# Attention scores on half arrays: K and Q loaded once, one bank for h, three for the attention's outputs

## The chip, the cores and the metric

The kernel runs on one core of one Trainium2 chip. The metric is the device time of one execution in microseconds (us). TensorE (PE) multiplies matrices, VectorE (DVE), ScalarE (ACT) and GpSimd (POOL) work on elements, and SyncE (SP) issues the DMA transfers. Each engine takes its instructions in a fixed order and stops at the first whose operands or buffers are not ready, so a late instruction holds all that stands behind it on its engine.

## The reference

Three layers follow one another. The first is attention over 4 batches of 8 heads, 576 positions and 64 columns a head. Scores below the row's maximum minus `tau` are dropped before the softmax. The two others are dense pairs of matrix products on 2304 tokens, 512 to 2048 to 512, each with its own activation between the products.

```python
scores = scale * np.matmul(q, k.transpose(0, 1, 3, 2))
thresh = np.max(scores, axis=-1, keepdims=True) - tau
scores = np.where(scores >= thresh, scores, -1000000000.0)
attn = np.exp(scores - np.max(scores, axis=-1, keepdims=True))
attn = attn / (np.sum(attn, axis=-1, keepdims=True) + 1e-09)
x = np.matmul(attn, v)            # rows of one token joined over the heads
...
h = x @ w_in                      # first layer: 512 -> 2048
sp = np.where(h > 20.0, h, np.log1p(np.exp(np.minimum(h, 20.0))))
x = (h * np.tanh(sp)) @ w_out     # 2048 -> 512
...
h = x @ w_in2                     # second layer
out = (h * np.clip(h + 3.0, 0.0, 6.0) / 6.0) @ w_out2
```

## The kernel before

**Parts of a number.** Accuracy beyond one 16-bit or one fp32r product is had by parts: an operand is written as a high part and the rest of it, a low part. For the dense layers both parts are f16, and a product is three matmuls (high times high, high times low, low times high; `TERMS`, line 36). For the scores the parts are fp32r.

**Attention.** Heads go in 16 pairs (4 batches, 4 pairs). A pair has four full query tiles of 128 rows for each head and one tail tile, which holds the last 64 rows of both heads: 9 score tiles of 128 x 576, so 144 in all; we count progress in these "heads". K and Q arrive with the 64 columns of a head stacked twice over the 128 partitions (`_stack`, line 1358). In `pair` (971) ACT makes the high parts (`k_hi` 991, `q_hi` 984), DVE the low part of K (`k_lo` 994, `kl` in the trace), and POOL the low part of Q into the other 64 rows (`q_lo` 987; the helper `sub`, line 330, holds the instruction). One matmul over 128 rows is then (high Q + low Q) times one part of K, so a head needs two matmuls for each of two halves of 288 columns (`scores`, 1044): 8 for a full tile of two heads, 8 for a tail tile.

**From scores to outputs.** For each head DVE takes the row maximum (`peak` 1066), ACT the exponential (`exp` 1076) and the threshold (`threshold` 1071), DVE masks (`mask` 1079, the last reader of the scores), ACT and POOL make the f16 parts (`p_hi` 1084, `p_lo` 1087), a DMA transposes them (1092), and PE multiplies with V (`pv` 1098). Scores lie in a ring `s` of two tiles of two PSUM banks each; a head takes one tile, and the next scores may enter it when its mask is done. Outputs and turned tiles share the ring `aux`, two banks.

**Dense work in the gaps.** When the first half of a batch is through, the first product of the first layer for that block of 256 tokens can begin (`inner` 679, `gemm1` 655): 8 groups of 24 matmuls (line 661, `h_g`), each into one of two banks of the ring `h`, emptied by `he_t` on ACT or DVE (`take`, 706) and stored. A block has 192 such matmuls. The weights of this product are converted during the first batch (`one_conversion` 493: lines 519 and 524 on DVE, 511 and 330 on POOL). The second product and the second layer (lines 825, 661 and 837) fill PE after the attention.

**What sets the order.** Nothing is scheduled on the chip. `Plan` (131) keeps a clock for every engine while the program is built, takes the task that can start first (within `WINDOW`, by due time) and writes its instructions down. The due times come from constants (`STEP`, `PREP_AHEAD`, `MOE_LAG`, `EASE`), the durations from literals in the tasks. They say nothing of the chip's time; they only set the order.

```python
r_s = ring("s", ps_a, BANKS["s"], [P, 2, 512])
r_aux = ring("aux", ps_a, BANKS["aux"], [P, FULL])
r_rk = ring("rk", ap, 1, [P, 2, S])
...
deps = [ql[j], kl] if c < NQ else [*ql, kl]
held = [s[j], qs, kd, kld]
```

Of the kernel before, what the change touches and what calls it, by code (L numbers as in the profile page):

```python
# [21 lines left out]
P = 128  # L22
# [19 lines left out]
STEP = 2.55  # L42
START = 7.2
PV_OFF = 6.17
PREP_AHEAD = 2.45
CONV_STEP = 1.5
CONV_AT = 3.0
LATE_STEP = 4.0
# [4 lines left out]
MOE_LAG = 8.26  # L53
RATE = 1.32
NX = 3
FLIP = 1.61
ALPHA = {"act": 3.07, "pe": 10.98}
# [5 lines left out]
MERGE_HI = False  # L63
MERGE_LO = True
# [5 lines left out]
PIECE = 4  # L70
LAG = 4
BANKS = {"s": 2, "aux": 2, "h": 2}
# [4 lines left out]
EASE = {"mk": -1.41, "ph": 1.68, "pl": -3.92, "tr": -1.06, "ex": 0.6, "s": -3.68, "th": -5.15}  # L77
P_LO = ("pool",)
EXPAND = {"act": 1.15}
BUFS = {"e": 3, "p16": 3}  # L80
LATE = {"gs": 5, "hl": 2, "xl": 2, "yl": 1, "h": 2, "y": 2}
WINDOW = {"pe": 0.05, "dve": 0.05, "act": 0.02, "pool": 0.15, "sp": 0.22}


class Ring:
# [11 lines left out]
    def when(self):  # L97
        return min(self.free)[0] if self.free else None
# [32 lines left out]
class Plan:  # L131
# [153 lines left out]
def fused_kernel(ctx: ExitStack, tc, q, k, v, tau, w1i, w1o, w2i, w2o, out):  # L285
# [393 lines left out]
    def inner(blk, early, at=None, gap=0.0):  # L679
# [19 lines left out]
        for fp in range(NG):  # L699
# [219 lines left out]
    r_qs = [Ring("qs", lambda i, name, k=k: qts[2 * k + i], 2) for k in range(2)]  # L919
# [51 lines left out]
    def pair(n, begin, values, sets):  # L971
# [8 lines left out]
        qs, kd, kld = Buf(r_qs[sets]), Buf(r_kd[sets]), Buf(r_kld[sets])  # L980
# [26 lines left out]
        a = prep({"act": 1.155}, lambda e: q_hi(slice(0, 2)), [lq], [rq, qs], "qh")
        for j in range(2):
            ql.append(prep(both(S), lambda e, j=j: q_lo(e, j), [a], [rq, qs], f"ql{j}_"))
        kl = prep({"dve": 1.42}, k_lo, [kh], [rk, kd, kld], "kl")  # L1010
# [15 lines left out]
        def query_tiles(t, c, o, i):  # L1026
# [17 lines left out]
            def scores(j):  # L1044
                if c < NQ:
                    q0 = j * TAIL + c * P
                    st = qs.tile[:, j, q0 : q0 + P]
                    terms = [(st, kd.tile[:, j]), (st, kld.tile[:, j])]
                else:
                    flat = qs.tile.rearrange("p a n -> p (a n)")  # L1050
                    terms = [
                        (flat[:, q0 : q0 + P], k.tile[:, jj])
                        for jj, q0 in enumerate((FULL, S))
                        for k in (kd, kld)
                    ]
                for half in range(2):
                    for m, (lh, rh) in enumerate(terms):
                        mm(  # L1058
                            s[j].tile[:, half, :HALF],
                            lh,  # L1060
                            rh[:, half * HALF : (half + 1) * HALF],
                            start=m == 0,
                            stop=m == len(terms) - 1,
                        )
# [50 lines left out]
            pks, exs = [], []  # L1115
            for j in heads:
                deps = [ql[j], kl] if c < NQ else [*ql, kl]
                held = [s[j], qs, kd, kld]
                a = go(
                    {"pe": 0.56 if c < NQ else 1.08}, lambda e, j=j: scores(j), deps + [prev[0]],  # L1120
                    held, "s", j,
                )
                prev[0] = a
                a = go({"dve": 0.75}, lambda e, j=j: peak(j), [a], [s[j], neg], "pk", j)
# [29 lines left out]
            a = go({"sp": 0.7}, transpose, parts, [p16, pt], "tr", w - 1, 1.0 * w, 0.0, [prev[2]])  # L1154
# [159 lines left out]
    r_hp.grow(maker(ps2, "hp", [P, 2 * BLK], F32), LATE["h"])  # L1314
# [93 lines left out]
```

## Time and profile before

| what | us |
|---|---|
| median of 3 runs (1085.86 to 1089.76) | 1089.45 |
| the profiled execution | 1089.44 |
| its span, first to last instruction | 1087.7 |
| PE busy | 968.7 |
| DVE busy | 604.3 |
| ACT busy | 605.1 |
| POOL busy | 469.2 |

The profiled execution lasts 1.7 us longer than its span, and it is as long as the median, so a sum made against the span's stages can be set beside the runs as it stands. The shares of busy time are averages over stages that differ: attention with its preparation until 453 us, a first product that runs out until 503 us, and then dense products alone. Waits are read stage by stage.

### The profile page before, as it was taken

The page shows a single profiled execution, that of the slowest core. Times are in us where ns is not written, and L with a number is a line of the kernel's source. Part 1 is how long each engine was busy: PE and PEld are TensorE (multiplying, and loading weights), DVE is VectorE, ACT ScalarE, POOL GpSimd, SP SyncE. Part 2 cuts the span into 40 slices and gives each one's busy share as a digit, 9 for nine tenths or more (in the row PEclk, how much of TensorE's full clock was granted, in tenths as well). Part 3 has the DMA queues.
Part 4 walks back from the last instruction along what each step waited for, and adds up shares of the span by engine and source line. Part 5 has one row for each costly group of instructions (what it writes and reads, how often), then busy time and mean ns, then how long its engine had stood idle before and what let it go on. Part 6 is the DMA issues. An engine that isn't in the chain of part 4 may idle for free.

```text
span 1087.7 us, 21597 instructions
## 1 busy us (share of the span) xinstructions
PE 968.7 (89%) x8839; PEld 784.4 (72%) x8839; DVE 604.3 (56%) x1068; ACT 605.1 (56%) x982; POOL 469.2 (43%) x408
## 2 busy tenths in 40 slices
PE   2447688898999986979999999999999999999997
PEld 1436577787899875868888888886666667666663
DVE  7778997777787779757679678621211111111110
ACT  6637777787788778546676559522322322223322
POOL 3859766466565658634433025512222222222221
PEclk9856789998999998999999999999999999999999
DMA  6867679999999898966576967410100100100001
GB/s 258 209 172 175 139 191 238 221 229 252 195 219 218 179 227 171 239 236 235 192 233 231 335 230 265 140 40 1 58 29 11 40 30 11 40 20 20 20 1 39
DMA packets 199394, 162.87 MB, mean 150 GB/s; under 512 B 174080, under 2 KB 174080, under 8 KB 194176
## 3 DMA queue, kind: packets, MB, share of 16 engines
q1 hardware_dynamic: 199296, 161.51, 55.7%
q8 instruction: 69, 1.13, 0.4%
q14 instruction: 29, 0.24, 0.1%
HBM read 90.18 MB, written 28.84 MB: 109 GB/s over the span
## 4 chain that ended last, share of the span: by engine, by line
PE 71%; DMA 11%; DVE 8%; POOL 4%; ACT 3%; issue 2%; SPq 0%; ACTq 0%; POOLq 0%; DVEq 0%
PE h_g L661 19%; PE y_y L825 17%; PE y_y L837 17%; DMA pt_tr<-p_ph 9%; PE hp_g L661 9%; PE s_s L1058 4%; PE aux_pv L1106 4%; DVE e_ex L1080 2%; POOL p_ph L330 2%; DVE nm_pk L1067 1%; POOL qs L330 1%; DMA v_lv<-in_v 1%; ACT e_ex L1077 1%; DMA rq_lq<-in_q 1%; DMA raw_lr<-in_moe_w_in 1%
## 5 line engine op out<-in xcount | busy, mean ns | idle before, releaser
L661 PEld LDWEIGHTS <-w 128*128 128x128 f16 x3456 | 333.5, 98 | 66.9 <-issue 5.8
L330 POOL TENSOR_TENSOR p_ph<-e_ex,p_ph 128x128 f16<-128x128 f32 (+3 forms) x160 | 195.2, 1242 | 110.3 <-ACT p_ph L1085 69.0
L330 POOL TENSOR_TENSOR gs_h<-hl_r,gs_h 128x512 f16<-128x512 f32 x72 | 83.5, 1159 | 286.2 <-ACT gs_h L800 286.2
L837 PE MATMUL y_y<-w,gs_h 128*128 128x512 f16 x864 | 201.7, 379 | 0.0
L825 PE MATMUL y_y<-gs_h,w 128*128 128x256 f16 x1728 | 191.7, 273 | 0.0
L661 PE MATMUL h_g<-x_fl,w 128*128 128x256 f16 x1536 | 187.6, 275 | 3.2 <-ACT he_t L709 2.4
L825 PEld LDWEIGHTS <-w 128*128 128x128 f16 x1728 | 168.4, 98 | 19.3
L837 PEld LDWEIGHTS <-gs_h 128*128 128x128 f16 x864 | 84.5, 98 | 82.0
L800 ACT ACTIVATE gs_h<-hl_r 128x512 f16<-128x512 f32 x72 | 45.3, 629 | 172.0 <-PE y_y L837 155.4
L1067 DVE TENSOR_REDUCE nm_pk<-s_s 128x1 f32<-128x576 f32 x144 | 105.8, 751 | 35.3 <-PE s_s L1058 34.4
L1080 DVE SCALAR_TENSOR_TENSOR e_ex<-s_s,thr_th,e_ex 128x576 f32<-128x576 f32 x144 | 111.6, 810 | 15.0 <-ACT thr_th L1072 11.1
L1106 PE MATMUL aux_pv<-vh,pt_tr 128*128 128x65 f16 (+1 forms) x1296 | 91.1, 207 | 29.8 <-DMA pt_tr<-p_ph 28.1
L1077 ACT ACTIVATE e_ex<-s_s,nm_pk 128x576 f32<-128x576 f32 x144 | 104.1, 732 | 18.4 <-DVE nm_pk L1067 16.3
L784 DVE SCALAR_TENSOR_TENSOR hl_r<-hl_r,f,h_g 128x512 f32<-128x512 f32 x36 | 26.9, 747 | 156.2 <-ACT hl_r L778 156.2
L1106 PEld LDWEIGHTS <-pt_tr 128*128 128x128 f16 x2016 | 83.8, 105 | 37.6 <-DMA pt_tr<-p_ph 33.3
L1085 ACT ACTIVATE p_ph<-e_ex 128x576 f16<-128x576 f32 x144 | 95.6, 680 | 25.7 <-DVE e_ex L1080 18.6
L784 DVE SCALAR_TENSOR_TENSOR hl_r<-hl_r,f,hp_g 128x512 f32<-128x512 f32 x36 | 26.9, 746 | 145.3 <-ACT hl_r L778 145.3
L661 PE MATMUL h_g<-xl_x,w 128*128 128x256 f16 x864 | 104.3, 273 | 0.0
L661 PE MATMUL hp_g<-xl_x,w 128*128 128x256 f16 x864 | 103.0, 273 | 0.0
L1058 PE MATMUL s_s<-kda_kh,qs 128*128 128x288 f32 x200 | 68.5, 357 | 26.8 <-DVE e_ex L1080 18.3
L1058 PEld LDWEIGHTS s_s<-kda_kh,qs 128*128 128x128 f32 x200 | 43.2, 216 | 37.0 <-POOL qs L330 14.9
L804 DVE SCALAR_TENSOR_TENSOR gs_h<-hp_e,fscales,gs_h 128x512 f16<-128x512 f32 x72 | 52.6, 744 | 25.8 <-ACT gs_h L798 25.6
(321 smaller groups left out, 1297.0 us busy)
## 6 DMA issues: line engine op xcount, KB each, us to landing
hd<-he_t SPq DMA_DIRECT2D x36, 512.0 KB, 3.3
hl_l<-hd SPq DMA_DIRECT2D x36, 512.0 KB, 4.5
raw_lr<-in_moe_w_in SPq DMA_DIRECT2D x16, 1024.0 KB, 5.5
raw_lr<-in_moe_w_out SPq DMA_DIRECT2D x16, 1024.0 KB, 6.6
rk_lk<-in_k SPq DMA_DIRECT2D x16, 576.0 KB, 5.2
rq_lq<-in_q SPq DMA_DIRECT2D x16, 576.0 KB, 5.1
raw_lw<-in_moe_w_out SPq DMA_DIRECT2D x8, 1024.0 KB, 7.3
v_lv<-in_v SPq DMA_DIRECT2D x16, 320.0 KB, 4.6
```

Source lines behind the costliest of these rows:

```text
L330: engine[e].tensor_tensor(dst, a, b, ALU.subtract)
L661: mm(hv[:, j, :], wj[:, wl, c * P : (c + 1) * P], x.tile[:, c, xl, :], start=j == 0 and n == 0, stop=j == 1 and n == 11, skip_group_check= ...
L784: nc.vector.scalar_tensor_tensor(half(g), half(g), wsc[2]["f"][:, fp : fp + 1], h.tile, ALU.min, ALU.mult)
L804: nc.vector.scalar_tensor_tensor(s.tile[:, 1], gv(), fs[:, fp : fp + 1], s.tile[:, 0], ALU.mult, ALU.subtract)
L825: mm(yv[:, h, :], wt[m2][f // 2][:, f % 2, wl, c * P : (c + 1) * P], gs[fp].tile[:, gl, f % 2, :], start=fp == 0 and n == 0, stop=fp == NG ...
L837: mm(y.tile[:, j], gs[fp].tile[:, gl, f % 2, j * P : (j + 1) * P], wt[m2][f // 2][:, f % 2, wl, :], start=fp == 0 and n == 0, stop=fp == N ...
L1058: mm(s[j].tile[:, half, :HALF], lh, rh[:, half * HALF : (half + 1) * HALF], start=m == 0, stop=m == len(terms) - 1,)
L1067: nc.vector.tensor_reduce(neg.tile[:, j : j + 1], sv(j), AX.XY, ALU.max, negate=True)
L1077: nc.scalar.activation(ev(j), sv(j), AF.Exp, bias=neg.tile[:, j : j + 1])
L1080: nc.vector.scalar_tensor_tensor(ev(j), sv(j), thr.tile[:, j : j + 1], ev(j), ALU.is_ge, ALU.mult)
L1085: nc.scalar.activation(p16.tile[:, js, :S], e_.tile[:, js], AF.Copy)
L1106: mm(ov[:, dst, :d], pt.tile[:, j, ch, :], part.tile[:, src, vc, :], start=i == j == ch == 0 and part is vh, stop=j == w - 1 and ch == 8, ...
```

## The change

K and Q are loaded once (128 partitions, the two heads of a pair above each other) instead of twice. The parts now lie side by side as columns of one tile: `qs[:, 0]` and `qs[:, 1]` are the high and the low Q of both heads, `kd[:, 0]` and `kd[:, 1]` the same of K. A score matmul of a full tile reads 64 partitions, the upper ones for one head and the lower ones for the other, and `TERMS` makes three products of it (the product of the two low parts goes). The matmuls of the two heads alternate. A tail tile keeps matmuls over 128 partitions, on a Q of which each head's half is zero elsewhere: three terms, two halves, six matmuls. Both heads' scores are one task, which takes both tiles of `s`.

Around it: K is scaled in place on ACT, its low part may be made on POOL or DVE, the raw K and Q have two buffers each, `h` has one bank during the attention (a second one is added after it), `aux` three. The constants of the plan are new.

```diff
-STEP = 2.55
+STEP = 2.33
-PREP_AHEAD = 2.45
+PREP_AHEAD = 3.29
-MOE_LAG = 8.26
+MOE_LAG = 3.41
...
-BANKS = {"s": 2, "aux": 2, "h": 2}
+BANKS = {"s": 2, "aux": 3, "h": 1}
...
-    r_rq = ring("rq", ap, 1, [P, 2, S])
-    r_rk = ring("rk", ap, 1, [P, 2, S])
+    r_rk = ring("rk", ap, BUFS["r"], [P, S])
+    r_qs = [ring("qs" + "ab"[k], (ap, ep)[k], 2, [P, 2, QW], F32R) for k in range(2)]
     r_kd = [ring("kd" + "ab"[k], (ap, ep)[k], 2, [P, 2, S], F32R) for k in range(2)]
-    r_kld = [ring("kld" + "ab"[k], (ap, ep)[k], 2, [P, 2, S], F32R) for k in range(2)]
...
+        def load_q(e):
+            for j, r in enumerate(side):
+                nc.sync.dma_start(out=rq.tile[r, : S - j * TAIL], in_=q[n][r, : S - j * TAIL])
+            nc.sync.dma_start(out=rq.tile[D:, S:], in_=q[n][D:, FULL:])
+        def q_hi(e):
+            nc.scalar.activation(qs.tile[:, 0], rq.tile, AF.Copy)
+        def q_lo(e):
+            sub(e, qs.tile[:, 1], rq.tile, qs.tile[:, 0].bitcast(F32))
+        def k_scale(e):
+            nc.scalar.activation(rk.tile, rk.tile, AF.Copy, scale=qscale)
         def k_hi(e):
-            nc.scalar.activation(kd.tile, rk.tile, AF.Copy, scale=qscale)
+            nc.scalar.activation(kd.tile[:, 0], rk.tile, AF.Copy)
         def k_lo(e):
-            nc.vector.scalar_tensor_tensor(
-                kld.tile, rk.tile, qscale, kd.tile.bitcast(F32), ALU.mult, ALU.subtract
-            )
+            sub(e, kd.tile[:, 1], rk.tile, kd.tile[:, 0].bitcast(F32))
...
-            def scores(j):
-                if c < NQ:
-                    q0 = j * TAIL + c * P
-                    st = qs.tile[:, j, q0 : q0 + P]
-                    terms = [(st, kd.tile[:, j]), (st, kld.tile[:, j])]
+            def scores(e):
...
+                cols = slice(c * P, (c + 1) * P)
                 for half in range(2):
-                    for m, (lh, rh) in enumerate(terms):
+                    for m, (qi, ki) in enumerate(TERMS):
+                        for j, r in enumerate(side):
+                            mm(
+                                s[j].tile[:, half, :HALF],
+                                qs.tile[r, qi, cols],
+                                kd.tile[r, ki, half * HALF : (half + 1) * HALF],
+                                start=m == 0,
+                                stop=m == 2,
+                            )
...
+            prev[0] = scored = go(
+                {"pe": S_COST}, scores, [ql, kl, prev[0]], [*s, qs, kd], "s"
+            )
             for j in heads:
...
     r_hp.grow(maker(ps2, "hp", [P, 2 * BLK], F32), LATE["h"])
+    r_h.grow(maker(ps2, "hx", [P, 2 * BLK], F32), 2 - BANKS["h"])
```

The order moves at three places. The first is PE at a full score tile. In the names, `s_s2_3_0` is pair 2, tile 3, head 0; in the changed kernel the digit before the last number tells the head. Before, the two heads stand behind each other:

```order
L1106 MATMUL aux_pv1_2_0_1_1206<-vh1_132,pt_tr1_2_1_1_1124 128x65
L1058 MATMUL s_s2_3_0_0_1249<-kdb_kh2_1_300,qs2_134 128x288
L1058 MATMUL s_s2_3_0_0_1249<-kldb_kl2_2_361,qs2_134 128x288
...
L1058 MATMUL s_s2_3_1_0_1257<-kdb_kh2_1_300,qs2_134 128x288
L1058 MATMUL s_s2_3_1_0_1257<-kldb_kl2_2_361,qs2_134 128x288
...
L1106 LDWEIGHTS pt_tr1_3_1_1_1197
```

In the changed kernel, at tile 1 of pair 6:

```order
L668 MATMUL h_g20_0_0_0_1_1991<-x_fl0_0_2_504,w0_2_155 128x256
L1074 MATMUL s_s6_1_0_0_2032<-kdb_kh6_1_1391,qsb_qh6_1_1383 128x288
L1074 MATMUL s_s6_1_0_1_2033<-kdb_kh6_1_1391,qsb_qh6_1_1383 128x288
...
L1074 MATMUL s_s6_1_0_1_2033<-kdb_kh6_1_1391,qsb_qh6_1_1383 128x288
L668 LDWEIGHTS w0_3_156
L668 MATMUL h_g30_0_0_0_1_2047<-x_fl0_0_2_504,w0_3_156 128x256
```

The matmuls of the two heads (`s_s6_1_0_0` and `s_s6_1_0_1`) now alternate, each with 64 rows of the same K and Q tiles, 12 in one run where there were 8.

The second is DVE between the masks (`e_ex`) of the 11th and 12th head and the next row maximum (`nm_pk3_0`), where the fourth pair comes in. `cvt` is a weight conversion, `kldb_kl3` the low part of K. Before:

```order
L1080 SCALAR_TENSOR_TENSOR e_ex2_1_0_2_524<-s_s2_1_1_0_515,thr_th2_1_0_1_530,e_ex2_1_0_2_524 128x576
L937 TENSOR_REDUCE vt_vm0_1_1_293<-v_lv2_1_0_496 128x1
...
L524 SCALAR_TENSOR_TENSOR cvt_c0_1__1_412<-raw_lr0_1_0_177,cvt_c0_1__1_412 128x1024
L519 SCALAR_TENSOR_TENSOR cvt_c0_2__1_588<-raw_lr0_2_0_491,cvt_c0_2__1_588 128x1024
L995 SCALAR_TENSOR_TENSOR kldb_kl3_2_633<-rk_lk3_0_375,qscale_84,kdb_kh3_1_433 128x1152
L524 SCALAR_TENSOR_TENSOR cvt_c0_2__1_588<-raw_lr0_2_0_491,cvt_c0_2__1_588 128x1024
L1016 SCALAR_TENSOR_TENSOR vlb_vl3_3_671<-v_lv3_0_0_169,vs_ve0_1_184,vh3_140 128x640
L1177 TENSOR_SCALAR den_dt2_0_2_676<-aux_pv2_0_0_1_593 128x4
L1067 TENSOR_REDUCE nm_pk3_0_0_1_679<-s_s3_0_0_0_666 128x1
```

In the changed kernel:

```order
L1096 SCALAR_TENSOR_TENSOR e_ex2_1_0_2_566<-s_s2_1_0_0_544,thr_th2_1_0_1_570,e_ex2_1_0_2_566 128x576
L1096 SCALAR_TENSOR_TENSOR e_ex2_1_0_2_566<-s_s2_1_0_1_545,thr_th2_1_0_1_570,e_ex2_1_0_2_566 128x576
L531 SCALAR_TENSOR_TENSOR cvt_c0_1__1_349<-raw_lr0_1_0_185,cvt_c0_1__1_349 128x1024
L371 TENSOR_REDUCE top0_144<-aux_zp0_2_1_581 128x1
L408 TENSOR_SCALAR top0_144<-top0_144 128x1
L409 TENSOR_SCALAR sc0_145<-top0_144 128x1
L412 TENSOR_SCALAR sc0_145<-sc0_145 128x1
L1083 TENSOR_REDUCE nm_pk3_0_0_1_636<-s_s3_0_0_0_585 128x1
```

Of 16 instructions between the mask and the row maximum, with four conversion steps and the low part of K, five are left, with one conversion step; the low part of K stands on POOL.

The third is PE between two groups of the first product, `h_g50` and `h_g60` (weights `w0_5`, `w0_6`). Before, at block 1:

```order
L1106 MATMUL aux_pv6_0_0_1_2326<-vh2_136,pt_tr6_1_1_1_2319 128x65
L661 LDWEIGHTS w0_5_160
L661 MATMUL h_g50_0_0_1_1_2397<-x_fl0_2_2_1154,w0_5_160 128x256
...
L661 LDWEIGHTS w0_6_161
L661 MATMUL h_g60_0_0_1_1_2488<-x_fl0_2_2_1154,w0_6_161 128x256
...
L1058 MATMUL s_s4_3_0_0_2507<-kda_kh4_1_937,qs0_126 128x288
```

In the changed kernel, at block 0:

```order
L668 MATMUL h_g50_0_0_0_1_2217<-x_fl0_0_2_504,w0_5_158 128x256
L1233 MATMUL aux_fl5_0_1_2277<-ident_75,xn_dn5_0_2_2265 128x128 x2
L1122 LDWEIGHTS pt_tr6_0_1_1_2148
L1122 MATMUL aux_pv6_0_0_1_2280<-vh2_136,pt_tr6_0_1_1_2148 128x65
...
L668 LDWEIGHTS w0_6_159
L668 MATMUL h_g60_0_0_0_1_2314<-x_fl0_0_2_504,w0_6_159 128x256
...
L1074 MATMUL s_s4_2_0_0_2322<-kda_kh4_1_941,qsa_qh4_1_935 128x288
```

Before, the next group followed the last matmul of the one before at once, into the other bank. Now a turned tile (`aux_fl5`) and a whole product with V (`aux_pv6`, 28 matmuls) stand between them, while the one bank is emptied.

## Rows read from the trace of the kernel before

**Rows 1.** Page, busy time of the engines: busy us (share) x instructions

```profile
PE 968.7 (89%) x8839; PEld 784.4 (72%) x8839; DVE 604.3 (56%) x1068; ACT 605.1 (56%) x982; POOL 469.2 (43%) x408
```

**Rows 2.** Windows: stage, length, busy us (x instructions) PE PEld DVE ACT POOL, clock, DMA, GB/s

```profile
0.00:184.00 184.00, 109.48 (x1049) 94.97 (x1050) 153.14 (x262) 121.87 (x199) 122.63 (x112) 0.81 0.77 194
184.00:375.00 191.00, 176.52 (x2194) 162.01 (x2192) 146.33 (x259) 153.92 (x280) 115.34 (x97) 0.97 1.02 220
375.00:503.00 128.00, 104.01 (x1137) 91.44 (x1136) 96.20 (x192) 84.56 (x142) 75.85 (x63) 0.96 0.83 209
503.00:1000.00 497.00, 497.00 (x3952) 385.77 (x3950) 198.17 (x344) 221.49 (x329) 137.69 (x123) 1.00 0.33 114
```

**Rows 3.** Windows of line 1080 alone, the masks on DVE: busy us (x masks)

```profile
0.00:184.80 184.80, 37.30 (x48) 0.82 0.77 194
184.80:375.00 190.20, 54.97 (x71) 0.97 1.02 220
```

**Rows 4.** Timeline of DVE, 50 to 71 us: start us, us, engine line operation, idle before

```profile
50.35 0.76 DVE L1067 TENSOR_REDUCE nm_pk<-s_s 128x1 f32<-128x576 f32 x1 [0.20 <-PE s_s L1058]
...
65.07 2.31 DVE L995 SCALAR_TENSOR_TENSOR kldb_kl<-rk_lk,qscale,kdb_kh 128x1152 fp32r<-128x1152 f32 x1
67.30 2.18 DVE L524 SCALAR_TENSOR_TENSOR cvt_c__1_588<-raw_lr,cvt_c__1_588 128x1024 uint32<-128x1024 uint32 x1
...
70.27 0.74 DVE L1067 TENSOR_REDUCE nm_pk<-s_s 128x1 f32<-128x576 f32 x1
```

**Rows 5.** Costliest groups by shape: busy us, mean ns | idle before, releaser

```profile
L661 PE MATMUL h_g<-x_fl,w 128*128 128x256 f16 x1536 | 187.6, 275 | 3.2 <-ACT he_t L709 2.4 <-DVE top L364 0.8
L1085 ACT ACTIVATE p_ph<-e_ex 128x576 f16<-128x576 f32 x144 | 95.6, 680 | 25.7 <-DVE e_ex L1080 18.6 <-DMA pt_tr<-p_ph 4.7 <-DVE xn_dn L1184 1.0
L330 POOL TENSOR_TENSOR qs<-rq_lq,qs 64x576 fp32r<-64x576 f32 x32 | 46.9, 1466 | 27.5 <-ACT qs L985 26.2
L709 ACT ACTIVATE he_t<-h_g,hin 128x512 f32<-128x512 f32 x65 | 44.5, 684 | 23.3 <-PE h_g L661 19.6 <-DMA hd<-he_t 2.5 <-ACT xtail L1196 0.6
L985 ACT ACTIVATE qs<-rq_lq 128x1152 fp32r<-128x1152 f32 x16 | 18.5, 1159 | 3.4 <-DMA rq_lq<-in_q 3.4
L995 DVE SCALAR_TENSOR_TENSOR klda_kl<-rk_lk,qscale,kda_kh 128x1152 fp32r<-128x1152 f32 x10 | 14.3, 1427 | 0.3 <-ACT kda_kh L992 0.3
L992 ACT ACTIVATE kda_kh<-rk_lk,qscale 128x1152 fp32r<-128x1152 f32 x10 | 12.5, 1248 | 0.3 <-PE s_s L1058 0.2
L995 DVE SCALAR_TENSOR_TENSOR kldb_kl<-rk_lk,qscale,kdb_kh 128x1152 fp32r<-128x1152 f32 x6 | 9.4, 1574 | 0.8 <-ACT kdb_kh L992 0.8
```

**Rows 6.** Timeline of PE, 302 to 307 us

```profile
302.36 2.35 PE L661 MATMUL h_g<-x_fl,w 128*128 128x256 f16 x20
304.46 0.38 PE L1058 MATMUL s_s<-kda_kh,qs 128*128 128x288 f32 x1
304.68 0.29 PE L1058 MATMUL s_s<-klda_kl,qs 128*128 128x288 f32 x1
...
306.00 0.29 PE L1058 MATMUL s_s<-klda_kl,qs 128*128 128x288 f32 x1
306.14 0.20 PE L1106 MATMUL aux_pv<-vh,pt_tr 128*128 128x65 f16 x1
306.18 0.20 PE L1106 MATMUL aux_pv<-vlb_vl,pt_tr 128*128 128x64 f16 x1
```

**Rows 7.** Timelines of PE, DVE and ACT: one tile, 232 to 238 us

```profile
232.70 0.38 PE L1058 MATMUL s_s<-kdb_kh,qs 128*128 128x288 f32 x1
233.51 1.42 DVE L1067 TENSOR_REDUCE nm_pk<-s_s 128x1 f32<-128x576 f32 x2 [0.94 <-PE s_s L1058]
235.03 0.29 ACT L1072 ACTIVATE thr_th<-nm_pk,ntau 128x2 f32<-128x2 f32 x1
235.66 1.53 DVE L1080 SCALAR_TENSOR_TENSOR e_ex<-s_s,thr_th,e_ex 128x576 f32<-128x576 f32 x2
237.46 0.38 PE L1058 MATMUL s_s<-kdb_kh,qs 128*128 128x288 f32 x1
```

More of the change, by code (lines that the diff above doesn't have):

```diff
@@ L95, in grow, with when @@
             self.free.append((0.0, len(self.free), make, i))
-    def when(self):
-        return min(self.free)[0] if self.free else None
+    def when(self, n=1):
+        return sorted(f[0] for f in self.free)[n - 1] if len(self.free) >= n else None
     def take(self):
@@ L176, in _start @@
         t = task.ready[e]
+        wanted = {}
         for b in task.bufs:
             if b.slot is None:
-                w = b.ring.when()
+                n = wanted[b.ring] = wanted.get(b.ring, 0) + 1
+                w = b.ring.when(n)
                 if w is None:
@@ L719, in inner @@
                 h_stored[blk, fp // 2] = task(
-                    {"sp": 0.5}, put, taken, [he], f"s{fp}", 2.0, fp + VECTOR
+                    {"sp": 0.5}, put, taken, [he], f"s{fp}", HD_DMA, fp + VECTOR
                 )
@@ L905, in fused_kernel @@
     r_xts = ring("xts", ap, 1, [P, TAIL])
-    vts, xtail, qts = [], [], []
+    vts, xtail, rqs = [], [], []
+    for i in range(BUFS["r"]):
+        rqt = ap.tile([P, QW], F32, name=f"rq{i}")
+        nc.gpsimd.memset(rqt[:D, S:], 0.0)
+        nc.gpsimd.memset(rqt[D:, FULL:S], 0.0)
+        rqs.append(rqt)
+    r_rq = Ring("rq", lambda i, name: rqs[i], BUFS["r"])
     for i in range(4):
         pool = ap if i < 2 else ep
-        qt = pool.tile([P, 2, QW], F32R, name=f"qs{i}")
-        nc.gpsimd.memset(qt[:, 0, S:].bitcast(F32), 0.0)
-        qts.append(qt)
         vt = pool.tile([P, 2, NQ + 1, D + 1], F16, name=f"vh{i}")
@@ L1007, in pair @@
[L1007 to L1010, printed above, removed]
+        a = prep({"act": 0.68}, k_scale, [lk], [rk], "kh")
+        a = prep({"act": 0.68}, k_hi, [a], [rk, kd], "kh")
+        kl = prep(K_LO, k_lo, [a], [rk, kd], "kl")
+        a = prep({"act": 0.68}, q_hi, [lq], [rq, qs], "qh")
@@ L1012, in v_hi @@
+        ql = prep(both(QW), q_lo, [a], [rq, qs], "ql")
         def v_hi(e):
@@ L1042, in ev @@
                 return e_.tile[:, j].rearrange("p (a n) -> p a n", a=2)
-            def scores(j):
-                if c < NQ:
-                    q0 = j * TAIL + c * P
-                    st = qs.tile[:, j, q0 : q0 + P]
-                    terms = [(st, kd.tile[:, j]), (st, kld.tile[:, j])]
[L1049 to L1055, printed above, removed]
-                for half in range(2):
-                    for m, (lh, rh) in enumerate(terms):
[L1058 to L1064, printed above, removed]
+            def scores(e):
+                if c == NQ:
+                    for half in range(2):
+                        for m, (qi, ki) in enumerate(TERMS):
+                            mm(
+                                s[0].tile[:, half, :HALF],
+                                qs.tile[:, qi, FULL:],
+                                kd.tile[:, ki, half * HALF : (half + 1) * HALF],
+                                start=m == 0,
+                                stop=m == 2,
+                            )
+                    return
+                cols = slice(c * P, (c + 1) * P)
+                for half in range(2):
+                    for m, (qi, ki) in enumerate(TERMS):
+                        for j, r in enumerate(side):
+                            mm(
+                                s[j].tile[:, half, :HALF],
+                                qs.tile[r, qi, cols],
+                                kd.tile[r, ki, half * HALF : (half + 1) * HALF],
+                                start=m == 0,
+                                stop=m == 2,
+                            )
             def peak(j):
@@ L1115, in query_tiles @@
             pks, exs = [], []
+            prev[0] = scored = go(
+                {"pe": S_COST}, scores, [ql, kl, prev[0]], [*s, qs, kd], "s"
+            )
             for j in heads:
[L1117 to L1124, printed above, removed]
+                a = go({"dve": 0.75}, lambda e, j=j: peak(j), [scored], [s[j], neg], "pk", j)
                 pks.append(a)
```

38 lines of the change are left out of this document (15 added, 23 removed).

## The prediction

> **What bounds the kernel now.** I read the windows by stage first, then PE's share in each, then DVE's, then the timeline of one tile.
>
> From 503 us PE has no gap at all: 497.00 us busy of 497, at full clock [rows 2]. So the end is the time at which PE has done all its work, and every microsecond is either PE work or a PE wait before 503 us. Over the span the waits are 1087.7 - 968.7 = 119 us [rows 1], and they lie in three stages [rows 2]: 74.5 us before 184, 14.5 from 184 to 375, 24 from 375 to 503.
>
> Before 184 us the limit is DVE: 153.1 us busy of 184 (83%), more than any other engine, and in this stage only 48 heads pass [rows 2, 3], 3.8 us each. The worst hole lies between two row maxima at 50.35 and 70.27 us: for 20 us no new head starts, while DVE does weight conversions and, between two of them, K's low part for the fourth pair, 2.31 us long [rows 4].
>
> From 184 to 375 us it is 71 heads in 190.2 us, 2.68 a head or 24.1 a pair of 9 [rows 3]. PE is busy 92%, DVE 77%, ACT 81% [rows 2]. PE is close to its limit but waits for single things.
>
> **The change part by part.**
>
> *Scores on PE.* At full clock a score matmul starts 0.133 us after the one before: (306.00 - 304.68) / 10 [rows 6]. Now a full tile has 8, a tail tile 8: 1.06 us each. After, a full tile has 12 in 6 pairs, a tail 6. No row shows a matmul on 64 rows. If the two of a pair go side by side, a pair costs one slot, 0.80 us a tile; if one waits for the other, 1.60. Over 64 full and 16 tail tiles that is 80 x -0.27 = -21 us, or 64 x 0.54 - 16 x 0.27 = +30 us. I take -21. The rows let a matmul start long before the one ahead has left (0.29 us long, 0.133 apart), so what a matmul holds is its rows of the array, its operands' partitions and its bank. The two of a pair share none of these. At the low clock before 184 us (granted 0.81 there [rows 2]) the saving is rather larger, and I leave that out.
>
> The first matmul after an f16 one takes 0.22 us to the next instead of 0.133 [rows 6]. The number of score runs on PE falls from 95 to 78, so this costs nothing more, if nothing else is paid where the array changes from 128 rows to 64.
>
> *DVE.* The 16 low parts of K go: 14.3 + 9.4 = 23.7 us [rows 5]. Up to the 48th head that is 8 of them, 8 x 1.5 = 12 us, and three bank emptyings that move to ACT (the order has them), at some 0.7 us each: 14 us. The conversions up to there stay 16, but only 7 of these steps instead of 11 stand before the 24th head. The hole before the 13th head [rows 4] keeps one conversion step of four and no K. At 83% busy, 14 us of work would be 17 us of time. I take 15; the bounds are 0 (something else is late there) and 20 (the whole hole).
>
> *POOL and ACT.* POOL now makes 32 low parts of Q of 1.466 us, 46.9 us [rows 5]. After, it makes 16 of Q over 640 columns (1.466 x 640/576 = 1.63) and 16 of K over 576 (1.47): 49.6 us. POOL is 67% busy at most [rows 2], so 3 us more are covered, but if POOL were late, its transposed parts would be too. ACT gives up 16 x (1.16 + 1.25) = 38.6 us and gets 16 x (0.68 + 0.68 + 0.76) = 33.9 us, from 0.68 us for 576 columns [rows 5]; seven more bank emptyings at 0.684 us make up for it. Nothing.
>
> *Loads.* K and Q bring half the bytes, and a second raw buffer lets the next pair's load go before the last low part is made. Q now takes three issues on SP, 32 more in all, before transposes queued there. I cost both at nothing: the DMA engines are busy 0.77 of the first stage and 1.02 of the second [rows 2], where fewer bytes can only help. If SP holds the transposes back, it is part of the second rival.
>
> *One bank for h.* Between two groups of 24 there must now be 0.68 us of ACT [rows 5] and the ways to it and back. The order puts work between all of the groups during attention (before, 29 of 48 followed at once), mostly a product with V. I take 0; a wait of 0.3 us at each of 50 groups would be 15 us, covered only where PE would wait anyway. Today PE waits 3.2 us in all before the largest set of these matmuls [rows 5]. The third bank for the outputs takes waits away, if anything.
>
> *Both heads' scores at once.* They need both tiles of the ring, so the next scores wait for the second mask. In one tile of today the scores begin at 232.70, the first maximum at 233.51 after four matmuls [rows 7]; with six pairs it is 1.08 us. Then two maxima 1.42, threshold 0.10 + 0.29, masks 0.11 to 0.34 later and 1.53 long, and 0.27 to the next scores: 4.8 to 5.0 us a full tile. A tail tile, with one maximum and one mask, takes 3.3 us and starts beside the last mask of the tile before (0.77): 2.6. A pair is then 21.8 to 22.6 us, under today's 24.1: this wait becomes the next limit, but does not slow the stage.
>
> *Dense work moved.* When the 48th head starts, PE's order holds 72 matmuls of the first product instead of 224; at the 120th 1036 instead of 1032. So 152 matmuls x 0.105 us (2.10 us for 20 [rows 6]) = 16 us move out of the first stage into the second. There PE had 176.5 us of work; it gets +16 and, for 8 pairs, -8 x 5 x 0.27 = -11: 182 of 191 us. It fits, with waits of 9 instead of 14.5 us. I let this stage keep its length.
>
> *Sum.* First stage -15, second 0 with the dense work caught up, third three pairs x 1.35 = -4. The profiled execution, 1089.4 us, is as long as the median: 1089.4 - 19 = 1070. By PE's work: 21 us less of it and about the same waits, which agrees.
>
> **The rivals.**
>
> *Slower: the halves go one after the other.* Full tiles then cost 1.60 us instead of 1.06. It decides from 0.094 us a matmul on: 64 x (12 x 0.094 - 1.06) is what the tails save. PE's work grows by 30 us, and the chain of a tile by 0.8 to 5.6 us or more, a pair to 25 or more against 24.1. Time 1089 + 30 = 1119. For it: PE's order alternates strictly, and no row shows two at once. Against: the operands and banks are disjoint.
>
> *No change: the locks eat it.* PE has one bank for h and both score tiles taken together; if each tile of the second stage keeps today's waits on top of 5.0 us, a pair stays at 24 to 25 us, and what the first stage gains goes into the 16 us of dense work caught up later. PE's saved 21 us become waits. Time 1085 to 1094. For it: 48 heads of DVE relief buy time in which PE has nothing to do. Against: 8% of waits are there to be used.
>
> A change of the array's rows may itself cost. A product with V is 0.20 us long at 0.03 to 0.04 us a start [rows 6]; if PE must empty itself at both ends of 64 runs, 128 x 0.16 = 20 us are lost, and the time is again 1089. The Trainium skill says in "TensorEngine Tiling (Array Packing)", section Tiling Modes, that changing the tiling mode drains the engine. All matmuls of this trace use 128 rows, so no run here shows it yet.
>
> *More: the plan's waits shrink.* If pairs come down to the chain, 22.5 us each over the last 96 heads (10.7 pairs), 1.6 x 10.7 = 17 us more are gained. Time 1053. For it: every engine but POOL has less to do. Against: PE's 182 us of work in the second stage leave room for 9.
>
> **How the numbers follow.** My forecast has 0.60 with its own range of 1058 to 1083; the halves in turn 0.10; the locks or drains 0.19; more 0.11. About 0.5% (5.4 us) is what a measurement of this kernel can tell from no change. Faster by that is below 1084: 0.60 + 0.11 and a little of the third case, 0.73. Same, 0.15, is the third case. Slower, 0.12, is the second and the tail of the third. The range from 1050 to 1090 takes in the "more" case and most of the locks, and leaves out the halves in turn.
>
> **What would show it.** In the profile after: score matmuls of a tile in pairs that start within some 0.02 us of each other, 0.13 us a pair (right) or 0.13 us each (wrong). No low part of K on DVE, and no hole near 60 us; the 48th mask near 170 us. The second stage at 24 us a pair or a little less. PE's idle time in it at `he_t` near zero. The prediction is wrong if PE busy falls by 20 us and its waits rise by as much, or if the first stage is no shorter.

## The result, and the profile after

The changed kernel takes 1073.46 us (median of 4 runs, 1071.8 to 1076.39) against 1088.36 (4 runs, 1085.86 to 1089.76): ratio 0.9869, 95% interval 0.9839 to 0.9898, or 14.9 us less. The forecast was 1070 us in a range of 1050 to 1090, faster. The profiled execution is the slowest of the four, 1076.39 us, with a span of 1074.6, 13.1 us under the span of before.

The busy times on the page of the changed kernel, which answer to [rows 1]:

```profile
PE 968.0 (90%) x9063; PEld 769.3 (72%) x9063; DVE 586.0 (55%) x1044; ACT 601.3 (56%) x1006; POOL 463.9 (43%) x408
```

PE is as busy as before, 968.0 against 968.7. The forecast wanted 21 us less. What shrank is the time in which PE does nothing: 1074.6 - 968.0 = 106.6 us instead of 119 (some 6 us of either lie after PE's last matmul, at the end of the span). The same stretches as in [rows 2], of the changed kernel:

```profile
0.00:184.00 184.00, 113.06 (x1226) 94.48 (x1227) 153.11 (x279) 130.91 (x228) 132.04 (x122) 0.82 0.82 191
184.00:375.00 191.00, 182.58 (x2370) 159.72 (x2367) 136.31 (x244) 150.34 (x292) 108.66 (x93) 1.00 0.98 200
375.00:503.00 128.00, 106.56 (x1128) 90.69 (x1126) 88.02 (x169) 79.31 (x132) 68.40 (x57) 0.93 0.67 186
503.00:1000.00 497.00, 497.00 (x3935) 384.12 (x3934) 199.56 (x342) 219.54 (x326) 138.62 (x124) 1.00 0.32 110
```

From 503 us to its last matmul PE has no gap in either kernel, so the end still follows from what was done before. Fixed times cut both kernels at different places of their work, so I count by masks. The masks alone, as in [rows 3]:

```profile
0.00:167.70 167.70, 37.10 (x48) 0.81 0.80 189
```

The 48th mask ends at 167.6 us instead of 184.7: 17.1 us earlier. The whole first stage up to it, before and after (columns as in [rows 2]):

```profile
0.00:184.70 184.70, 110.18 (x1055) 95.61 (x1056) 153.84 (x263) 122.57 (x199) 122.91 (x112) 0.82 0.77 194
0.00:167.60 167.60, 96.66 (x1009) 80.55 (x1010) 140.37 (x254) 119.23 (x207) 122.11 (x113) 0.81 0.80 189
```

DVE has 13.5 us less work here, and its idle time falls from 30.9 to 27.2 us. K's 8 low parts alone were 12.4 us of that work. From there to the 120th mask, and on to the 144th, first in the kernel before:

```profile
184.70:381.60 196.90, 181.26 (x2234) 166.04 (x2231) 150.02 (x265) 157.01 (x287) 118.66 (x98) 0.97 1.03 219
381.60:444.90 63.30, 48.27 (x600) 42.87 (x601) 52.95 (x95) 47.50 (x86) 45.57 (x36) 0.95 0.95 206
```

and in the changed kernel:

```profile
167.60:364.60 197.00, 189.80 (x2459) 166.07 (x2455) 141.80 (x254) 154.55 (x298) 114.56 (x98) 1.00 0.97 200
364.60:433.50 68.90, 55.54 (x692) 45.99 (x693) 53.30 (x99) 48.77 (x89) 44.09 (x36) 0.90 0.81 174
```

The second stage is as long as it was, 197.0 against 196.9, though PE does 8.5 us more in it: its waits fall from 15.6 to 7.2. The third is 5.6 us longer, and the rest 1.7 shorter. So the whole gain arises in the first stage, and the later ones give back a part of it: -17.1 + 0.1 + 5.6 - 1.7 = -13.1.

PE at a full tile, to be read beside [rows 6]:

```profile
301.42 0.22 PE L1122 MATMUL aux_pv<-vla_vl,pt_tr 128*128 128x128 f16 x1
301.47 0.40 PE L1122 MATMUL aux_pv<-vh,pt_tr 128*128 128x130 f16 x4
301.80 1.07 PE L1074 MATMUL s_s<-kdb_kh,qsb_qh 64*128 64x288 f32 x12
302.80 1.37 PE L668 MATMUL h_g<-x_fl,w 128*128 128x256 f16 x11
```

Twelve matmuls in 1.07 us, of which one takes 0.29 to 0.40: the two of a pair do go side by side. Their single records start 1 to 9 ns apart in this run, and a pair follows the last after 0.133 us (0.235 the first). But six pairs are 0.80 us, and from the first score to the next `h_g` it is 1.00. Take the runs between 160 and 400 us whose neighbours are `h_g` on both sides. In the changed kernel 0.202 us pass from the start of the last `h_g` to the first score and 0.996 from there to the next `h_g` (medians of 22 runs); in the kernel before, with eight matmuls, 0.028 and 1.144 (4 runs). Less the slot of that `h_g` itself, 0.109, a full tile costs 1.09 us against 1.06. Eight slots of 0.133 explain all of the 1.06, six pair slots 0.80 of the 1.09; the other 0.29 lie at the two ends of the run, where PE goes from 128 rows to 64 and back.

DVE where the hole was [rows 4]:

```profile
49.46 1.22 DVE L531 SCALAR_TENSOR_TENSOR cvt_c__1_349<-raw_lr,cvt_c__1_349 128x1024 uint32<-128x1024 uint32 x1
...
51.36 1.41 DVE L1083 TENSOR_REDUCE nm_pk<-s_s 128x1 f32<-128x576 f32 x2
...
56.90 1.41 DVE L1083 TENSOR_REDUCE nm_pk<-s_s 128x1 f32<-128x576 f32 x2
```

The row maxima follow each other after 5.5 us; the 20 us without one are gone, and no gap before the 48th mask is longer than 8.0 us. The groups that answer to [rows 5]:

```profile
L668 PE MATMUL h_g<-x_fl,w 128*128 128x256 f16 x1536 | 186.4, 276 | 5.8 <-ACT he_t L716 5.0 <-DVE top L371 0.8
L1074 PE MATMUL s_s<-kda_kh,qsa_qh 64*128 64x288 f32 x480 | 56.9, 352 | 17.2 <-DVE e_ex L1096 13.0 <-POOL kda_kh L337 1.8 <-ACT kda_kh L1009 1.5
L337 POOL TENSOR_TENSOR qsa_qh<-rq,qsa_qh 128x640 fp32r<-128x640 f32 x10 | 16.1, 1613 | 8.8 <-ACT qsa_qh L1000 8.8
L337 POOL TENSOR_TENSOR kda_kh<-rk_lk,kda_kh 128x576 fp32r<-128x576 f32 x10 | 14.1, 1413 | 0.0
```

K's low parts are POOL's (the six others in `kdb` too), at 1.41 us where 1.47 was estimated, Q's at 1.61 (1.63). The one bank costs PE 5.0 us of waits at `he_t` instead of 2.4, most of it after the attention (4.6 us from 433.5 us on, below), 0.5 in the second stage.

### The profile page after: what moved, and what is told of

It is laid out like the page before. It is cut to its first block, busy times and chain, and to the rows that moved or that the text cites. A ratio compares the mean times of both kernels' runs of the same rounds, so it can differ in the third digit from the quotient of the medians.

```text
span 1074.6 us, 22033 instructions
## 1 busy us (share of the span) xinstructions
PE 968.0 (90%) x9063; PEld 769.3 (72%) x9063; DVE 586.0 (55%) x1044; ACT 601.3 (56%) x1006; POOL 463.9 (43%) x408
## 4 chain that ended last, share of the span: by engine, by line
PE 77%; DVE 8%; DMA 6%; ACT 4%; issue 2%; POOL 1%; SPq 0%; ACTq 0%; DVEq 0%; POOLq 0%
PE h_g L668 23%; PE y_y L832 18%; PE y_y L844 17%; PE hp_g L668 9%; PE s_s L1074 5%; DMA pt_tr<-p_ph 5%; PE aux_pv L1122 4%; DVE e_ex L1096 3%; DVE nm_pk L1083 2%; ACT e_ex L1093 1%; PE s_s L1062 1%; POOL p_ph L337 1%; ACT he_t L716 1%; DMA hd<-he_t 1%; PE aux_fl L1233 1%
## 5 line engine op out<-in xcount | busy, mean ns | idle before, releaser
L337 POOL TENSOR_TENSOR p_ph<-e_ex,p_ph 128x128 f16<-128x128 f32 (+3 forms) x160 | 188.4, 1199 | 133.3 <-issue 102.9
L807 ACT ACTIVATE gs_h<-hl_r 128x512 f16<-128x512 f32 x72 | 45.3, 630 | 167.6 <-PE y_y L844 164.5
L1096 DVE SCALAR_TENSOR_TENSOR e_ex<-s_s,thr_th,e_ex 128x576 f32<-128x576 f32 x144 | 111.5, 811 | 27.3 <-ACT thr_th L1088 15.6
L1083 DVE TENSOR_REDUCE nm_pk<-s_s 128x1 f32<-128x576 f32 x144 | 103.0, 752 | 35.7 <-PE s_s L1074 31.2
L1122 PE MATMUL aux_pv<-vh,pt_tr 128*128 128x65 f16 (+1 forms) x1296 | 92.8, 209 | 22.5 <-DMA pt_tr<-p_ph 19.2
L1122 PEld LDWEIGHTS <-pt_tr 128*128 128x128 f16 x2016 | 87.6, 106 | 28.2 <-DMA pt_tr<-p_ph 26.3
L1101 ACT ACTIVATE p_ph<-e_ex 128x576 f16<-128x576 f32 x144 | 94.5, 683 | 12.8 <-DVE e_ex L1096 9.3
L1074 PE MATMUL s_s<-kda_kh,qsa_qh 64*128 64x288 f32 x480 | 56.9, 352 | 17.2 <-DVE e_ex L1096 13.0
L1074 PEld LDWEIGHTS s_s<-kda_kh,qsa_qh 64*128 64x128 f32 x480 | 42.9, 218 | 39.8 <-issue 23.0
L716 ACT ACTIVATE he_t<-h_g,hin 128x512 f32<-128x512 f32 x72 | 49.2, 685 | 30.4 <-PE h_g L668 25.8
```

Of the source, the lines that this page charges most:

```text
L337: engine[e].tensor_tensor(dst, a, b, ALU.subtract)
L716: nc.scalar.activation(dst, h.tile, AF.Copy, scale=f)
L1074: mm(s[j].tile[:, half, :HALF], qs.tile[r, qi, cols], kd.tile[r, ki, half * HALF : (half + 1) * HALF], start=m == 0, stop=m == 2,)
L1083: nc.vector.tensor_reduce(neg.tile[:, j : j + 1], sv(j), AX.XY, ALU.max, negate=True)
L1096: nc.vector.scalar_tensor_tensor(ev(j), sv(j), thr.tile[:, j : j + 1], ev(j), ALU.is_ge, ALU.mult)
L1101: nc.scalar.activation(p16.tile[:, js, :S], e_.tile[:, js], AF.Copy)
```

## The experiments

Three theories stood against each other: (a) the gain is the lighter first stage, and PE's saved score work is eaten where the array's rows change; (b) it is the new order alone, whatever the scores do; (c) it is PE's score work, which the busy times above already speak against. Times are medians; the ratio is to the kernel before, which measured 1088.1 to 1089.1 beside them.

**What a change of rows costs.** In the changed kernel a 64-column matmul over all 128 rows is put between the two halves of a full tile (two more changes of rows), and, for control, the same matmul ahead of the run (none more). The order is that of the changed kernel.

```diff
 for half in range(2):
+    if half:
+        mm(s[0].tile[:, 1, :TAIL], ones, ones[:, :TAIL], start=True, stop=True)
```

> The changed kernel with one small matmul over all 128 rows (64 columns, its result is overwritten) between the two halves of each full tile's run: two more changes between 64 and 128 rows a tile. Theory, from the changed kernel's trace (first score matmul 0.20 us after an f16 one instead of 0.03, the next f16 one 0.22 us after the last instead of 0.135): each pair of changes costs some 0.26 us, so a run grows by 0.26 us and the small matmul, PE by some 19 us: 1085 to 1093 us. Rival, what was read as a change of rows is only the tail of two streams: the run grows by the small matmul alone, 0.03 to 0.06 us: 1074 to 1077 us.

> Control of the split run: the same small matmul over all 128 rows, but ahead of each full tile's first score matmul, where the rows change anyway. Both theories: no more changes, PE grows by 64 x 0.03 = 2 us: 1073 to 1077 us.

Measured: 1085.45 us (ratio 0.9992, 0.9972 to 1.0011) split, 1077.14 (0.9901, 0.9876 to 0.9926) with the matmul ahead. The page's busy times, split:

```profile
PE 993.8 (92%) x9127; PEld 779.8 (72%) x9127; DVE 582.6 (54%) x1044; ACT 601.0 (55%) x1006; POOL 467.2 (43%) x408
```

and with the matmul ahead:

```profile
PE 974.3 (91%) x9127; PEld 777.9 (72%) x9127; DVE 584.4 (54%) x1044; ACT 600.0 (56%) x1006; POOL 468.5 (44%) x408
```

The same instructions, and 19.5 us more PE. This sum mixes granted clocks (the first stage had 0.73 in one profile, 0.79 in the other), so the price is read where both had 1.00, from the 48th to the 120th mask, split first:

```profile
168.20:374.70 206.50, 200.49 (x2500) 170.47 (x2495) 140.68 (x254) 154.50 (x299) 114.60 (x98) 1.00 0.89 192
165.10:363.40 198.30, 190.99 (x2492) 168.84 (x2488) 141.94 (x254) 154.48 (x299) 114.72 (x98) 1.00 0.96 197
```

These are 32 full tiles: 9.5 us more PE, 0.30 a tile, and 8.2 us more time, close to the 8.3 us between the two medians. A split tile in the trace:

```profile
173.94 0.66 PE L1076 MATMUL s_s<-kdb_kh,qsb_qh 64*128 64x288 f32 x6
174.53 0.20 PE L1073 MATMUL s_s<-ones 128*128 128x64 bf16 x1
174.66 0.66 PE L1076 MATMUL s_s<-kdb_kh,qsb_qh 64*128 64x288 f32 x6
```

Between the last pair of one half and the second pair of the other lie 0.59 us instead of 2 x 0.133; 0.03 of that is the added matmul itself, as the control shows it. So two changes cost 0.29 to 0.30 us here, as in the changed kernel's own runs. (They change the number type as well; the runs of before do so too, and pay nothing beyond their eight slots.) That is (a)'s term: 64 x 0.29 = 18.6 us of PE work paid for 64 x 0.27 = 17 saved. The Trainium skill says in "TensorEngine Tiling (Array Packing)", section Tiling Modes, that changing the mode drains the engine; the trace agrees, with these 0.29 us for both changes of a run.

**The heads in turn.** The same 12 matmuls, head 0's six ahead of head 1's.

```diff
-for half in range(2):
-    for m, (qi, ki) in enumerate(TERMS):
-        for j, r in enumerate(side):
+for j, r in enumerate(side):
+    for half in range(2):
+        for m, (qi, ki) in enumerate(TERMS):
```

> The changed kernel, the six score matmuls of head 0 before the six of head 1, all else in the same order. Theory, from starts 3 ns apart in the changed kernel's trace: two matmuls go side by side because they use different rows of the array, so six on the same rows take a slot of 0.133 us each; a run grows from 0.77 to about 1.55 us, PE by 64 x 0.78 = 50 us, of which the 7 us of waits in the second stage hide little: 1110 to 1125 us. Rival, PE finds pairs whatever the order, or the slots are set by something that both share: same time as the changed kernel, 1073.

Measured: 1084.06 us (0.997, 0.9952 to 0.9989). It lies between the theory and its rival, and the theory was far off in two ways. One tile in the trace:

```profile
305.29 1.43 PE L1074 MATMUL s_s<-kdb_kh,qsb_qh 64*128 64x288 f32 x12
306.66 0.61 PE L668 MATMUL h_g<-x_fl,w 128*128 128x256 f16 x4
```

First, the run takes 1.37 us to the next `h_g`, not 1.8: head 1's first matmul starts 0.38 us after head 0's first, beside its third or fourth, and three pairs still overlap. (In 51 of the 62 runs the matmul that announces head 0's scores as ready, the sixth as written, is the ninth of the twelve to start.) That is 0.37 us more a tile than alternating, where 0.78 was expected. Second, part of this work hides in waits. The second stage, between the 48th and the 120th mask:

```profile
165.60:368.90 203.30, 200.52 (x2474) 177.77 (x2471) 142.76 (x255) 155.69 (x300) 114.82 (x98) 1.00 0.92 194
```

PE works 10.7 us more in it, and it lasts 6.3 us longer: waits fall from 7.2 to 2.8. In the whole run PE is 30.6 us busier, a part of it because the granted clock of the first and the third stage was lower (0.77 instead of 0.81, 0.83 instead of 0.90), and the time grows by 10.6.

**The change without the price of the rows.** Low Q times high K is left out of the full tiles: 8 matmuls in 4 pairs, which was to take about as much off PE as the changes of rows put on.

```diff
-for m, (qi, ki) in enumerate(TERMS):
+for m, (qi, ki) in enumerate(TERMS[:2]):
...
-stop=m == 2,
+stop=m == 1,
```

> The changed kernel, with each score matmul run of a full tile cut from 12 to 8 matmuls (two products instead of three: low Q times high K is left out, so the scores lose accuracy); every engine's order stays as it was. It takes 64 x 4 starts in 64 x 2 pairs of 0.133 us away, 64 x 2 x 0.133 = 17 us of PE work, which is what the changes of the array's rows cost by the split-run test (64 x 0.26). So its time is about what the change would have given if a change of rows were free. Theory 'PE's work is the time': 1073 - 17 = 1056, PE idle near 107. Theory 'waits set the attention': in the run with the heads in turn 31 us of PE work cost only 11 us of time, so 17 us taken away give about a third: 1066 to 1069, PE busy near 951 and PE idle near 117 to 119.

Measured: 1064.56 us (0.9765, 0.9742 to 0.9789), 8.9 us under the changed kernel, just below the range of the theory of waits. But the reason is not that theory's. In the profiles PE is busy for 7.4 us less (968.0 to 960.6), where 17 were expected, and its idle time falls from 106.6 to 104.0 us, where that theory wanted 117 to 119 and the other 107. Less work came off than was counted, and what came off was not lost in waits. The second and the third stage:

```profile
163.40:354.10 190.70, 182.43 (x2328) 157.68 (x2326) 142.19 (x255) 154.46 (x298) 114.77 (x98) 1.00 0.95 207
354.10:423.30 69.20, 55.92 (x652) 46.36 (x653) 52.90 (x98) 48.74 (x89) 44.10 (x36) 0.83 0.84 173
```

In the second stage, at the same clock as in the changed kernel, 7.4 us of PE work less (32 tiles x 0.27 would be 8.5) are 6.3 us of time: there the work counts nearly in full. In the first stage 4.2 us are gained (48th mask at 163.4), in the third nothing (69.2 us, at a lower clock). So an estimate for changes of rows at no cost is about 1065; no run has the three products without the changes.

**Order and structure apart.** The kernel before with the changed kernel's constants of the plan, and the changed kernel with the old ones.

```diff
-STEP = 2.55
+STEP = 2.33
...
-MOE_LAG = 8.26
+MOE_LAG = 3.41
```

> The kernel before with the changed kernel's plan constants (due times, windows, transfer costs) and nothing else of the change: K and Q still doubled, eight score matmuls a tile, K's low part on DVE, two banks for h. Theory: the gain is made before the 48th head, by conversions that stand later (order) and by DVE being rid of K's low parts (structure), about half each: 1078 to 1084 us, 48th mask near 176 us. Rival A, the order is the whole gain: 1073. Rival B, the structure is the whole gain: 1088 or more.

> The changed kernel with the plan constants of the kernel before; structure, banks and buffers as changed. Theory: half of the gain stays, 1077 to 1084 us. Rival A, the order is the whole gain: 1088. Rival B, the structure is the whole gain: 1073.

Measured: 1096.81 (1.0085, 1.0053 to 1.0117) and 1096.6 us (1.0094, 1.0065 to 1.0122). Both expectations fell. At the 48th mask the first has half of the gain, the second a little over a third: 176.2 and 178.4 us against 184.7 and 167.6. But it is lost again. The second stage of the old kernel with the new constants:

```profile
176.20:378.70 202.50, 182.52 (x2248) 165.30 (x2244) 149.90 (x263) 156.50 (x289) 118.72 (x99) 0.98 0.97 213
```

and of the new kernel with the old constants:

```profile
178.40:379.00 200.60, 181.39 (x2321) 154.69 (x2319) 139.52 (x254) 151.25 (x290) 114.16 (x96) 0.97 0.88 189
```

PE waits 20.0 and 19.2 us there, against 7.2 with both. So the new constants alone bring no gain, which speaks against (b), and neither does the new structure alone. Each of the two runs also has a written order of its own, and what such an order can cost is measured below; so they do not tell what each half is worth.

**Single parts.** Two banks for `h` and two for the outputs; one and two (a bank unused); one raw buffer each for K and Q; K's low parts on DVE again. Each edit makes the plan write its order anew.

```diff
-BANKS = {"s": 2, "aux": 3, "h": 1}
+BANKS = {"s": 2, "aux": 2, "h": 2}
```

```diff
-BANKS = {"s": 2, "aux": 3, "h": 1}
+BANKS = {"s": 2, "aux": 2, "h": 1}
```

```diff
-BUFS = {"e": 3, "p16": 3, "r": 2}
+BUFS = {"e": 3, "p16": 3, "r": 1}
```

```diff
-K_LO = {"pool": 1.4, "dve": 0.72}
+K_LO = {"dve": 0.72}
```

> The changed kernel with two banks for h and two for the outputs, as before. Theory: the one bank costs PE only the 5.7 us that it waits at the emptying, so 1068 to 1076 us, no difference that counts. Rival, one bank for h is what keeps PE's waits from falling: 1060. Other rival, the third output bank is part of the gain: 1080 or more.

> The changed kernel with one bank for h and two (instead of three) for the attention's outputs, one bank unused; the plan writes a new order around it. Theory 'the third output bank is needed, since products with V, turned tiles and row sums stand between the groups of the one h bank': 1085 to 1097, as with two banks for each. Theory 'the one h bank suits the order, the third output bank is spare': 1072 to 1078.

> The changed kernel with one raw buffer for K and one for Q instead of two, so that the next pair's loads wait for the low parts of this one. Theory: the loads ahead are a part of the first stage's gain, 3 to 8 us: 1076 to 1082 us. Rival: the preparation is early enough without, 1073.

> The changed kernel with K's low part on DVE again, at half its old size. Theory: DVE is the limit of the first stage; 8 x 0.72 us there, at some 85% busy, are 7 us later, the 48th mask near 174 us: 1077 to 1082 us. Rival: POOL, which gets 1.4 us a pair less, is as much the limit: 1070 to 1075 us.

| run | us | ratio (95%) | 48th mask |
|---|---|---|---|
| two banks for h, two for outputs | 1096.52 | 1.0067 (1.0046 to 1.0089) | 170.8 |
| one and two | 1093.9 | 1.0047 (1.0029 to 1.0065) | 172.9 |
| one raw buffer | 1083.9 | 0.9958 (0.9945 to 0.9972) | 169.7 |
| K's low parts on DVE | 1085.46 | 0.9975 (0.9958 to 0.9993) | 172.9 |

All lose 10 to 23 us against the changed kernel. The run with two and two banks lies in the open range of its other rival (1080 or more), the run with one and two in that of its first theory; the two others lie above every range that was set for them, though the 48th mask of the last was expected near 174. Before these are read as prices of the edits, one has to know what a new order costs by itself.

**A new order alone.** The plan's own price of a score run from 0.85 to 0.86, then to the 1.1 us that it takes. No instruction, bank or buffer is edited.

```diff
-S_COST = 0.85
+S_COST = 0.86
```

> The changed kernel with the plan's own price of a score run raised from 0.85 to 0.86 us. No edit to any instruction, bank or buffer; only the order is written anew (two to four instructions change their engine). It measures what a new order alone does. Theory 'each of the edited kernels lost time because of its edit (fewer output banks, one raw buffer, K on DVE)': this one stays at 1071 to 1077. Theory 'the constants fit one order, and any other order that the plan writes loses': 1082 to 1095, with 10 to 13 us of PE waits after 510 us as in those kernels.

> The changed kernel with the plan's price of a score run set to what a run takes on the chip, 1.1 us instead of 0.85. Theory 'a truer price gives a better order': 1066 to 1072. Theory 'any other order loses': 1082 to 1095.

Measured: 1086.27 us (0.9976, 0.9959 to 0.9993) and 1091.15 (1.003, 1.001 to 1.005). So 0.01 in one constant costs 12.8 us, nearly the whole gain: the 14.9 us belong to the changed kernel in this one order, not to its structure alone. With 0.86 the attention ends even earlier, at 426.8 us instead of 433.5; the loss lies behind it. The rest of that run, from its 144th mask on:

```profile
426.80:1084.40 657.60, 631.67 (x4926) 478.25 (x4924) 244.95 (x444) 276.54 (x410) 182.02 (x163) 0.99 0.31 108
```

and of the changed kernel:

```profile
433.50:1074.60 641.10, 625.99 (x4913) 476.68 (x4910) 250.50 (x439) 278.79 (x414) 183.11 (x163) 1.00 0.32 110
```

16.5 us longer, 10.8 of them waits. PE's longest waits in these stretches (what waited, for what; total us, times, longest), with 0.86:

```profile
PE h_zp L368 <- ACT dgb_zd L363: 7.1, 3, 4.7
PE h_g L668 <- ACT he_t L716: 5.7, 4, 3.5
PE h_g L668 <- DVE top L371: 2.7, 6, 0.8
PE h_g L668 <- DVE he_t L718: 1.6, 1, 1.6
...
```

and in the changed kernel:

```profile
PE h_g L668 <- ACT he_t L716: 4.6, 5, 2.2
PE h_zp L368 <- ACT he_t L716: 3.6, 1, 3.6
PE h_g L668 <- DVE top L371: 1.1, 3, 0.4
```

So of the four single parts, none has a price that is told apart from the new order's, which is 12.8 and 17.7 us without any edit. With K on DVE the 48th mask is at 172.9 us, where the new order alone has 166.0 and 168.2. That would make the 8 low parts up to there worth about 5 us to the first stage, at the half size that the change gave them; on DVE they took 10.8 us together, not the expected 8 x 0.72 = 5.8. But the run with one and two banks, which leaves them on POOL, is at 172.9 too, so this is not shown. Whether the third output bank matters stays open. No run beat the changed kernel with all of its products.

Of the three theories (a) is left. Its price of the rows is measured; the lighter first stage is read from the profiles, and no run takes it alone out of the changed kernel in the same order.

## Why the prediction was right, and where it was not

*The first stage: -15, measured -17.1.* Right, with no hole near 60 us and the 48th mask at 167.6 (near 170). The reason holds: DVE lost 13.5 us of work up to there (forecast 14), and its idle time fell by the other 3.6. The order has its part in it: with the new structure and the old constants DVE has 10.5 us less work by the 48th mask than in the kernel before, but 4.2 us more idle time. How the 17.1 us divide between K's low parts and the order is not shown.

*Dense work moved: the second stage keeps its length.* Right as to the length, and this is what makes the first stage's gain last. By the 48th mask 97 matmuls of the first product had started, instead of 252; in the second stage it is 959 instead of 816, 143 x 0.105 = 15 us more. PE's work there should be 181.3 + 15.0 - 8 tails x 0.27 + 32 full tiles x 0.03 - 5.4 (an estimate: 3% for the granted clock of 1.00 instead of 0.97) = 189.7, and is measured as 189.8; the waits are 7.2 us where 9 were forecast. That there was room for the dense work is partly luck: the forecast made it with 11 us of saved score work, of which 1.2 came, and the clock, which was not in the forecast, gave 5.4.

*Scores on PE: -21. This is the step that failed.* The pairs are side by side as forecast, but "if nothing else is paid where the array changes from 128 rows to 64" did not hold: 0.29 us a run. What is left of the 21 us is 16 x 0.27 = 4.3 from the tails, less 64 x 0.03 = 1.9 that the full tiles now take more. PE's busy time stayed, and the cross-check in the sum ("21 us less of it and about the same waits") came to the right time from two wrong numbers: 0.7 us less work and 12.4 us less waiting. In the sum itself this term stood in the third stage, and in the second as the room for the dense work. (The 119 us of waits, said to lie in the three stages, are 113 there; the other 6 lie after PE's last matmul.)

*The third stage: -4, measured +5.6, and -1.7 after it.* Wrong by 8 us. Without cheaper full tiles there was next to nothing to gain; 41 more matmuls of the first product fell in it (4.3 us), and the granted clock was 0.90 instead of 0.95. No run tells these two apart.

*POOL, loads, SP, one bank, both heads at once: nothing.* Consistent with the second stage, whose waits fell. PE's wait of the scores for the mask there, which was to be the next limit, is 2.3 us at the tails and almost none at full tiles, in the waits of the changed kernel from 167.6 to 364.6 us:

```profile
PE s_s L1062 <- DVE e_ex L1096: 2.3, 4, 1.1
PE aux_pv L1122 <- DMA pt_tr<-p_ph: 1.2, 2, 0.9
PE h_g L668 <- ACT he_t L716: 0.5, 2, 0.3
PE s_s L1074 <- DVE den_dt L1192: 0.4, 1, 0.4
```

*The rivals.* The halves in turn were refuted by the pairs. The rival of the drains named 20 us, measured are 18.6, but set the time at 1089: it took them from a sum in which the score work hardly stood. With them the kernel gains 14.9 us; without them it would gain about 24, by the estimate from the run with two terms. What no case held is how much the written order decides: the forecast treated it as given, and 0.01 in one of its constants is worth 12.8 us. That the time came out 3.5 us from the forecast is therefore not proof of the sum: its first term held, its score term did not, and the stages after the 120th mask missed by 8 us.

## What to carry to other kernels

Packing two 64-row matmuls side by side halved their slots here, but each passage between full and half rows cost time: count the passages, and pack only where a run between two of them saves more than they cost (here 0.27 us a run was saved and 0.29 paid). Where one engine is at 96% in a stage and the order is written down ahead, ask first which work leaves the stage before it and whether the next has room for it. Before a single edit's time is called its price, move a constant that edits nothing and see what a new order alone does.

## What the runs showed of the hardware that was not expected

- Two fp32r matmuls on separate halves of the rows, 288 columns each, share a slot of 0.133 us. Written one head after the other they still overlap: by the spacing of the starts, the first matmul on the second half of the rows starts 0.38 us after the first on the first half, while matmuls written ahead of it have not started yet. So the fixed order in which each engine takes its instructions, as the text on the chip at the beginning has it, does not hold for the starts of matmuls on separate halves.
- Two changes of rows cost 0.29 us: the first score starts 0.202 us after a 256-column `h_g` (0.028 without a change of rows), 0.148 after a product with V (0.049), and the next f16 matmul 0.223 us after the last score (0.135).
- The granted clock of the third stage is not the same in kernels with one order: 0.90 in the changed kernel, 0.83 with two terms, where PE is busy for 55.9 us with fewer matmuls, against 55.5. What decides it was not tried.
